# A recurrent attention kernel: weight loading at the start, attention rows kept in SBUF, feed-forward slots shifted by one

## The chip, the cores and the metric

One core of a Trainium2 chip. The metric is device time in microseconds (us) of one launch; the medians below are over several runs. Shorter words used below: PE is TensorE, DVE VectorE, ACT ScalarE, POOL GpSimd, SP SyncE; a "q" behind a name (SPq) is that engine issuing DMAs.

## The reference

A sequence of 2048 rows of width 640 is cut into 64 segments of 32 rows. Each segment attends, in 32 heads of 128, to itself and to 8 memory rows, and the memory rows of its output are the next segment's memory. So the segments form a chain. A feed-forward layer with a squared relu follows; it depends on nothing but its own rows.

```python
for s in range(64):
    h = concat([mem, LN(x)[32*s : 32*s+32]])       # 40 rows
    q, k, v = h @ Wq, h @ Wk, h @ Wv               # 640 -> 32 heads x 128
    o = softmax(mask(q k^T * scale)) v             # 40 x 40 for each head
    o = o @ Wo                                     # 4096 -> 640
    mem = o[:8];  out_a[s] = o[8:]                 # mem goes to the next segment
h  = x + out_a
h2 = h + (relu(LN(h) @ w1 + b1) ** 2) @ w2 + b2    # hidden width 1728
```

Inputs and result are bf16.

## The kernel before

It works in 16 blocks of four segments (128 rows). PE's work in a segment is: projections q, k, v (`ps`), transposes (`pt`), scores (`pss`), softmax sums (`pz`), values (`po`), output projection (`pw`), and the small matmul that puts the new memory into place (`pm`). The last 8 rows of each segment ("tails") are needed by nobody in the chain; a block's tails are projected together (`pst`, `psw`). The feed-forward layer of block b-1 is cut into 8 "slots" (`psf`, `acc`) that fill the places in block b where PE would wait; its transposes are called `pth`.

The weights are laid out in four groups of 160 rows: 128 rows of each group make one full chunk of 128 partitions, and the four remainders of 32 rows together make the fifth chunk. The parts that the change touches:

```python
# start: fifth chunks go DRAM -> DRAM -> SBUF
for wi, src in enumerate((A_Wq, A_Wk, A_Wv)):
    nc.scalar.dma_start(out=w4s[wi].rearrange("(g r) f -> g r f", g=G),
                        in_=src.rearrange("(g q) h e -> g q (h e)", g=G)[:, 128:DG, :])
for wi, (w, src) in enumerate(((wq, A_Wq), (wk, A_Wk), (wv, A_Wv))):
    w2d = src.rearrange("d h e -> d (h e)")
    for c in range(4):
        nc.sync.dma_start(out=w[:, c, :], in_=w2d[c * DG:c * DG + 128, :])
    nc.sync.dma_start(out=w[:, 4, :], in_=w4s[wi])
wov = A_Wo.rearrange("h e d -> e h d")
for j in range(4):
    (nc.sync if j % 2 else nc.scalar).dma_start(out=wo[:, j * 8:(j + 1) * 8, :], in_=wov[:, j * 8:(j + 1) * 8, :])
# ... cut ...
# attention rows of the tails: 16 stores to DRAM for each block, read back by ff_rows
for g in range(G):
    for sp in range(4):
        r0 = b * 128 + sp * SEG + HD
        nc.sync.dma_start(out=a_rows[r0:r0 + TL, g * DG:(g + 1) * DG],
                          in_=ot[32 * g + sp * TL:32 * g + (sp + 1) * TL, :])
# ... cut: step(), the segment; the order of PE's work in it ...
half(wk, lhs, 1, kr, "dve")
run(first[2])
run(slots.get("k", ()))
run_ff("pv3")                                  # one feed-forward slot, or pth
turn(qr, qT[:, :, :, 0:SEG], "act", psum_v, "pv0")
turn(kr, kT[:], "dve", psum_v, "pv1")
# ... cut: scores, softmax ...
run_ff("pv0")                                  # one more slot
# ... cut: values ...
wo_units(lambda h: oT[:, h, 0:SEG], pw, 0, H)
o = wo_out(pw)
for g in range(G):
    nc.sync.dma_start(out=a_rows[s * SEG:s * SEG + HD, g * DG:(g + 1) * DG],
                      in_=o[32 * g + M:32 * g + SEG, :])
mem_to_hT(o, hT4s[(s + 1) // 4], (s + 1) % 4)  # pm
# ... cut ...
# last segment: feed-forward weights of the last block (fw, 4.4 MB) on SyncE's queue
if s == 4 * NB - 1:
    sl["q"].append(last_loads)
```

The softmax here doesn't subtract the row's maximum and nothing guards it: scores larger than these inputs give would overflow.

## Time and profile before

| quantity | value |
|---|---|
| median of the first five runs | 1302.75 us (1302.08 to 1305.56) |
| span of the profiled run | 1300.6 us, mean granted clock of PE 0.978 |
| first output projection (pw of segment 0) starts | 104.87 us |
| segments 1, 8, 60 and 63 start | 109.73, 236.49, 1186.13, 1238.82 us |
| one block in the body (segments 8 to 59, 13 blocks) | 73.05 us |

The page's lines are shown in the prediction.

### The profile page before, as it was taken

The page shows a single profiled execution, that of the slowest core. Times are in us where ns is not written, and L with a number is a line of the kernel's source. Part 1 is how long each engine was busy: PE and PEld are TensorE (multiplying, and loading weights), DVE is VectorE, ACT ScalarE, POOL GpSimd, SP SyncE. Part 2 cuts the span into 40 slices and gives each one's busy share as a digit, 9 for nine tenths or more (in the row PEclk, how much of TensorE's full clock was granted, in tenths as well). Part 3 has the DMA queues.
Part 4 walks back from the last instruction along what each step waited for, and adds up shares of the span by engine and source line. Part 5 has one row for each costly group of instructions (what it writes and reads, how often), then busy time and mean ns, then how long its engine had stood idle before and what let it go on. Part 6 is the DMA issues. An engine that isn't in the chain of part 4 may idle for free. (4 is left out here: it accounts for less than half of the span.)

```text
span 1300.6 us, 68304 instructions
## 1 busy us (share of the span) xinstructions
PE 1090.5 (84%) x31488; PEld 710.6 (55%) x31488; DVE 464.7 (36%) x987; ACT 414.7 (32%) x848; POOL 305.8 (24%) x981
## 2 busy tenths in 40 slices
PE   0058878999999999989999999999999999889865
PEld 0025545656566655656565555656565565556543
DVE  0003333344343434344333433344433434343411
ACT  0012323334343333334333333334333333334312
POOL 3001132222222222222221222222222222222213
PEclk9998989999999999999999999999999999999978
DMA  8840031222222222223222222223222232222250
GB/s 303 326 150 5 6 93 30 78 76 91 63 74 80 75 80 68 72 76 90 63 71 83 76 76 65 79 76 91 67 78 71 75 86 63 69 74 86 77 181 17
DMA packets 97576, 112.55 MB, mean 87 GB/s; under 512 B 30731, under 2 KB 94122, under 8 KB 95322
## 3 DMA queue, kind: packets, MB, share of 16 engines
q1 hardware_dynamic: 94078, 100.19, 25.2%
q8 instruction: 246, 4.03, 1.2%
q10 hardware_dynamic: 2140, 5.77, 1.2%
q0 software_dynamic: 1072, 2.23, 0.6%
q14 instruction: 40, 0.33, 0.1%
HBM read 102.88 MB, written 10.60 MB: 87 GB/s over the span
## 5 line engine op out<-in xcount | busy, mean ns | idle before, releaser
L208 PEld LDWEIGHTS <-hT 128*32 128x32 bf16 x7680 | 205.8, 97 | 185.0 <-issue 8.6
L227 PE MATMUL pw<-wo,oT 128*32 128x160 bf16 x8192 | 169.5, 239 | 44.4 <-issue 40.9
L227 PEld LDWEIGHTS <-oT 128*32 128x32 bf16 x8192 | 150.9, 100 | 67.2 <-issue 48.2
L208 PE MATMUL ps<-wv,hT 128*32 128x512 bf16 x2560 | 163.5, 383 | 0.0
L381 POOL TENSOR_TENSOR f<-ffr 128x128 bf16<-128x128 bf16 x224 | 84.7, 398 | 328.5 <-ACT ffr L379 277.6
L208 PE MATMUL ps<-wq,hT 128*32 128x512 bf16 x2560 | 155.0, 388 | 6.4 <-DVE hT L287 6.1
L208 PE MATMUL ps<-wk,hT 128*32 128x512 bf16 x2560 | 150.2, 380 | 0.0
L129 DVE CAST vr<-ps 128x512 bf16<-128x512 f32 x128 | 88.6, 692 | 71.9 <-PE ps L208 68.7
L379 ACT ACTIVATE ffr<-psf,b1f 128x128 bf16<-128x128 f32 x224 | 69.1, 359 | 91.8 <-PE psf L358 90.0
L129 DVE CAST qr<-ps 128x512 bf16<-128x512 f32 x64 | 44.3, 692 | 141.7 <-PE ps L208 141.7
L232 DVE CAST o<-pw 128x160 bf16<-128x160 f32 x64 | 20.8, 325 | 183.4 <-PE pw L227 173.3
L358 PE MATMUL psf<-hnT,w1c 128*128 128x128 bf16 (+1 forms) x1020 | 76.2, 220 | 9.5 <-DMA w1c<-w1d 9.5
L127 ACT COPY qT<-pt 128x1024 bf16<-128x1024 bf16 x64 | 64.8, 1012 | 58.1 <-PE pt L220 58.1
L451 POOL TENSOR_TENSOR p<-p,mask_t 128x128 bf16<-128x128 bf16 x64 | 27.5, 429 | 224.4 <-ACT p L444 224.4
L129 DVE CAST oT<-po 128x320 bf16<-128x320 f32 x128 | 56.9, 486 | 64.5 <-PE po L486 58.1
L127 ACT CAST qr<-ps 128x512 bf16<-128x512 f32 x64 | 37.5, 586 | 122.6 <-PE ps L208 122.6
L127 ACT CAST tq<-pst 128x512 bf16<-128x512 f32 x32 | 18.9, 591 | 178.2 <-PE pst L208 178.2
L358 PEld LDWEIGHTS <-w1c 128*128 128x128 bf16 (+1 forms) x1020 | 60.6, 99 | 26.6 <-issue 11.9
L370 PE MATMUL acc<-w2c,f 128*128 128x320 bf16 x404 | 72.8, 301 | 0.9 <-DMA w2c<-in_B_w_dram 0.8
L127 ACT CAST kr<-ps 128x512 bf16<-128x512 f32 x64 | 37.5, 586 | 102.5 <-PE ps L208 102.5
L127 ACT CAST oT<-po 128x320 bf16<-128x320 f32 x128 | 48.2, 429 | 68.3 <-PE po L486 68.3
L467 POOL TENSOR_TENSOR pn<-p,rk 128x128 bf16<-128x128 bf16 x64 | 42.8, 668 | 107.4 <-issue 80.8
(97 smaller groups left out, 1375.4 us busy)
## 6 DMA issues: line engine op xcount, KB each, us to landing
w1c<-w1d SPq DMA_DIRECT2D x190, 160.0 KB
w2c<-in_B_w_dram SPq DMA_DIRECT2D x188, 160.0 KB
wq<-in_A_Wq_dram SPq DMA_DIRECT2D x4, 1024.0 KB
wk<-in_A_Wk_dram SPq DMA_DIRECT2D x4, 1024.0 KB
wv<-in_A_Wv_dram SPq DMA_DIRECT2D x4, 1024.0 KB
a_rows<-o SPq DMA_DIRECT2D x256, 7.5 KB
a_rows<-o SPq DMA_DIRECT2D x256, 2.5 KB
xt<-in_A_x_dram SPq DMA_DIRECT2D x16, 160.0 KB
```

The costliest lines, as they stand in the source:

```text
L127: nc.scalar.copy(out=out_, in_=in_)
L129: nc.vector.tensor_copy(out=out_, in_=in_)
L208: nc.tensor.matmul(ps[32 * g:32 * g + 32, :], lhsT=lhs(c), rhs=w[:, c, g * EG + n * 512:g * EG + (n + 1) * 512], start=(c == 0), stop=(c = ...
L227: nc.tensor.matmul(ps[32 * g:32 * g + 32, 0:DG], lhsT=lhs(h), rhs=wo[:, h, g * DG:(g + 1) * DG], start=(h == 0), stop=(h == H - 1))
L232: nc.vector.tensor_copy(out=o[:], in_=ps[:, 0:DG])
L358: nc.tensor.matmul(ps[0:fs, j, :], lhsT=w1c[:, c, 0:fs], rhs=f["hnT"][:, c, :], start=(c == 0), stop=(c == DC - 1))
L370: nc.tensor.matmul(f["acc", hf][:, 0:320], lhsT=t1[0:k, :], rhs=w2c[0:k, hf * 320:(hf + 1) * 320], start=(fc == 0), stop=(fc == FC - 1))
L379: nc.scalar.activation(out=r[0:fs], in_=ps[0:fs, j, :], func=ACT.Relu, bias=b1f[0:fs, fc:fc + 1], scale=1.0)
L381: nc.gpsimd.tensor_tensor(out=t1[0:fs], in0=r[0:fs], in1=r[0:fs], op=ALU.mult)
L451: nc.gpsimd.tensor_tensor(out=p[:, :, NQ:NC], in0=p[:, :, NQ:NC], in1=mask_t[:, sp].unsqueeze(1).to_broadcast([128, HG, M + TL]), op=ALU.mult)
L467: nc.gpsimd.tensor_tensor(out=pn[:, :, NQ:NC].rearrange("p i (a q) -> p i a q", q=M), in0=p[:, :, NQ:NC].rearrange("p i (a q) -> p i a q", ...
```

## The change

Its intent: start the chain earlier, take single waits of PE away, and keep attention rows in SBUF instead of sending them through DRAM. Six parts, the diff cut to its core (left out: the loads of w1c and w2c are issued later within a segment, the last step of the feed-forward layernorm, `ff_apply`, moved from behind the q to behind the k projection, and some tail units are split otherwise):

```diff
@@ 1. start
-        for wi, src in enumerate((A_Wq, A_Wk, A_Wv)):
-            nc.scalar.dma_start(out=w4s[wi].rearrange("(g r) f -> g r f", g=G), ...)
+        load_x(1)                                  # second x block ahead of the weights
         ...
-            nc.sync.dma_start(out=w[:, 4, :], in_=w4s[wi])
+            for g in range(G):
+                nc.sync.dma_start(out=w[g * DR:(g + 1) * DR, 4, :], in_=w2d[g * DG + 128:(g + 1) * DG, :])
         ...
+        for j in (1, 3):
+            load_wo(j, nc.sync)                    # quarters 0 and 2: gpsimd, after the second block's transposes
@@ 2. attention rows
-                                nc.sync.dma_start(out=a_rows[r0:r0 + TL, g * DG:(g + 1) * DG],
-                                                  in_=ot[32 * g + sp * TL:32 * g + (sp + 1) * TL, :])
+                            stores.append(lambda eng, g=j // 4, sp=j % 4: eng.dma_start(
+                                out=rows_of(b)[sp * SEG + HD:(sp + 1) * SEG, g * DG:(g + 1) * DG], in_=...))
+                    sl["w"].append(lambda: run_stores(8, (nc.gpsimd,)))       # first segment of a block
+                        sl["q"].append(lambda b=b: (run_stores(8, (nc.gpsimd,)), ff_rows(b - 1)))   # second
@@ 3. w1 reformatted into w1d: ten GpSimd DMAs after block 0 become two in each of segments 0 to 6
+                for fc in range(2 * s, min(2 * s + 2, FC)):
+                    sl["w0"].append(lambda fc=fc: nc.gpsimd.dma_start(out=w1d[fc, :, :, 0:fs_of(fc)], ...))
@@ 4. feed-forward: pth behind pw of the third segment, slots one place later
-                        ffq.append(lambda tag, b=b: ff_turn(b - 1))
+                        sl["f"] = [lambda b=b: ff_turn(b - 1)]
+                    if sp == 3:
                         ffq.extend(lambda tag, b=b, p=p: ff_slot(b - 1, p, tag) for p in range(NP + 1))
@@ 5. fw: all its loads from sync to gpsimd
-                    sl["q"].append(last_loads)
+                    sl["k"].append(last_loads)
@@ 6. tail of the last block
-        ff_rows(NB - 1)
+        run_stores(16, (nc.sync, nc.scalar, nc.gpsimd))
-        for k in range(len(ffq)):
+        for k in range(2):
             run_ff(tags[k % 2])
         ff_stats(NB - 1)                           # its root now on ScalarE (Ln, Exp)
         ff_apply(NB - 1)
+        while ffq:
+            run_ff(tags[len(ffq) % 2])
         ff_turn(NB - 1)
```

## The prediction

> **What bounds the kernel now.** I read the page first, then the waits of TensorE (PE), then the order in time at the start, at one seam near 170 us and at the end. The page's busy shares and slices:
>
> ```profile
> PE 1090.5 (84%) x31488; PEld 710.6 (55%) x31488; DVE 464.7 (36%) x987; ACT 414.7 (32%) x848; POOL 305.8 (24%) x981
> PE   0058878999999999989999999999999999889865
> DMA  8840031222222222223222222223222232222250
> ```
>
> PE is busy 84%, every other engine under half. A slice is 32.5 us: PE is empty for two slices, nine tenths busy through the body, and sinks at the end. The body is a chain of 64 dependent segments, so only time in which PE stands still can be won. Who PE waits for, in total, times and longest:
>
> ```profile
> PE ptx L196 <- DVE xn L122: 58.4, 3, 33.3
> PE pw L227 <- issue: 40.9, 37, 1.7
> PE pth L343 <- DVE hn L122: 19.1, 15, 9.9
> PE pst L208 <- DMA wq<-w4s: 17.7, 1, 17.7
> ...
> PE psw L227 <- issue: 10.3, 9, 2.0
> PE psf L358 <- DMA w1c<-w1d: 9.5, 1, 9.5
> ...
> PE pss L437 <- POOL qT L416: 5.5, 1, 5.5
> ```
>
> Several are single events, so I placed them in time. The start:
>
> ```profile
> 53.43 0.89 DVE L105 BATCH_NORM_STATS2 lnst<-xt 128x6 f32<-128x320 bf16 x2 [27.28 <-DMA xt<-in_A_x_dram]
> ...
> 79.18 2.75 PE L208 MATMUL pst<-wq,hTt 128*32 128x512 bf16 x24 [17.71 <-DMA wq<-w4s]
> ```
>
> The second x block arrives at 53.4, because its load is queued behind all weights. Then PE does 16 matmuls and waits until 79.2 for the fifth chunk of wq, which goes DRAM to DRAM (w4s) and then into SBUF. The first output projection (pw) starts at 104.87. The seam after block 0, and the end:
>
> ```profile
> 163.67 1.25 POOL L589 DMA_DIRECT2D w1d<-in_B_w_dram  x1
> ...
> 172.56 0.39 PE L437 MATMUL pss<-qT,kTt 128*32 128x16 bf16 x32 [5.48 <-POOL qT L416]
> ```
>
> ```profile
> 1258.14 1.25 PE L358 MATMUL psf<-hnT,w1c 128*128 128x128 bf16 x10 [9.52 <-DMA w1c<-w1d]
> ...
> 1268.84 5.34 SPq L276 DMA_DIRECT2D a_rows<-o  x16
> ...
> 1278.46 0.49 DVE L328 TENSOR_TENSOR ffh<-ffa,ffh 128x640 bf16<-128x640 bf16 x1 [2.94 <-issue]
> ...
> 1284.60 0.71 PE L343 MATMUL pth<-ident,hn 128*128 128x128 bf16 x5 [9.86 <-DVE hn L122]
> ```
>
> Ten DMA issues on GpSimd hold up its copy of qT, and PE with it. In the last segment a small w1c load stands behind 4.4 MB of fw in the same queue. At the very end the attention rows travel to DRAM (16 stores of 0.33 us each) and back before the last layernorm can start, and its root takes 12 short GpSimd operations.
>
> **What the Trainium skill says.** "DMA: Bandwidth & Descriptors", section on why a DMA increments its semaphore by 16: the engines that share a transfer number the largest count up to 16 that divides the slowest dimension. The old w4s copy has 4 there, so 4 engines. The transfers of the first 60 us, in slices of 1.5 us, fit: the rate collapses around 13 to 17 us although megabytes are waiting, and reaches 410 to 437 later.
>
> ```profile
> GB/s 0 284 246 368 259 296 473 337 193 33 98 24 273 410 415 431 431 415 426 421 431 437 410 415 431 415 426 385 370 375 363 363 362 292 97 256 4 320 295 392
> ```
>
> "SBUF — State Buffer", section "Door 1: The DMA port swizzle": 32 partitions reach only 8 of 16 ports, measured 189 GB/s at 1 MiB. The new loads of the fifth chunks are 32 rows each. No transfer of the kernel before shows this. "DMA: Bandwidth & Descriptors", section "Queues, rings and completion order": an engine goes round robin between the queues, packet by packet. So fw on GpSimd's queue no longer stands ahead of w1c on SyncE's, it shares with it; the 9.5 us wait shows the old queueing. "Runtime: NRT & Kernel Launch", section "Instruction fetch mechanics": instructions come in 16 KiB blocks of 256. The page has 246 instruction packets for 4.03 MB, 16.4 KB each, and the places of the "pw <- issue" gaps, counted in PE's instructions, keep nearly one remainder of 256 from a gap to the next. The change keeps PE's instructions (62,978 before and after), so these some 51 us stay.
>
> **The change part by part.**
>
> 1. Start. Removed: the w4s copies, and the DRAM round trip of three fifth chunks. The second x block is loaded first. Two wo quarters move from ScalarE's queue to GpSimd's. PE's start: from the first bias cast (19.1) to the first layernorm's transposes took 5.6 us and the second x block needs some 6 more, so PE starts at 31 us, or as early as 25 if the bias lands sooner on engines that w4s no longer clogs. The wq work takes some 10 us (1.9 + 8.5 from the timeline), the wk work 8, two transposes 1. So PE wants wv at 44 to 50 us. When does it arrive? Bytes in queue order: xt 0.33 MB and three times 5.24 MB. At 0.42 MB/us the 12.9 MB of full-width loads take 31 us. The 3.15 MB of 32-row loads at an assumed 0.2 MB/us (estimate from the skill's SBUF page) take 16 us. With 2.5 us to start and some 3 us given to the two wo quarters, wv is complete near 53. From wv's fifth chunk to pw is some 8 us (95.53 to 104.87 before, less 1.0 for two transposes now done earlier). The last wo quarter should be in at about 60. So pw of segment 0 starts near 61 instead of 104.87: minus 44.
>
> 2. Seam at 170 us. The ten w1d issues (9 us together) become two per segment, after the oTt copy, where GpSimd is idle for several us. Minus 5.5, and minus 1 because the matmuls after the stall ran on a lowered clock (24 wv matmuls in 2.75 against 1.49 us).
>
> 3. Body, 14 blocks. The feed-forward transposes (pth) leave the place where they waited for hn and go behind pw in the third segment, and all slots of the feed-forward shift by one. PE's work is the same. Of 19.1 us of waits 9.9 are the last one, so 9.2 in 14 times, 0.65 each, vanish; the 0.3 us of transposes then lies inside the wait for the o copy (0.42 at that spot). Given back: the hnT eviction (0.49 us) on VectorE gets ahead of the hT copy, about +0.25, and the third segment keeps 8 instead of 12 filler matmuls ahead of pw, about +0.2. Net about 0.5 to 0.7 a block, minus 8. The 16 tail stores move to GpSimd in two lots of 8: at 0.54 us an issue (its small w1d issues) 4.3 us a lot, in stretches where GpSimd waits 5 us and more. I take nothing for them. Attention rows stay in SBUF; that was hidden, nothing.
>
> 4. Last segment. fw goes through GpSimd's queue (about 5 us of issue at 0.55 and 1.13 us apiece, finished before GpSimd's next mask). w1c shares the engines with fw: 640 KB at half of 0.4 MB/us and 2 us to land, against 5 us of room, so a wait of 0 to 2 us stays. pw then also runs at full clock (3.98 against 2.40 us). From its first matmul to the eviction of pw the segment takes 26.8 us now (1238.82 to 1265.65), the one before it 15.8 (1222.02 to 1237.83): 11.0 lost, of which I expect 9 back.
>
> 5. Tail. 16 stores over three queues (5 or 6 each, 2 to 3 us) straight into the SBUF tile, no reload; root by two ScalarE operations of about 0.25 us each instead of 3.8 us. From the end of the tail projection, 0.5 to evict, 2.7 to issue, 2 to land, 1.6 for add and statistics, 0.6 for the root: 7.5. But ScalarE's program order puts the root ahead of the relus of the slots that remain, so four slots follow it: 4.3 us, and pth starts at 11.8 after that point, before at 16.2. Minus 4.4.
>
> Sum: 44 + 6.5 + 8 + 9 + 4.4 = 72 to 74. 1302.75 minus 73.5 gives **1229 us**.
>
> **Rivals.** First: the start is bound by something else. For it: 21.4 MB (weights, wo and x) must come through the same engines, nothing here makes that less than 51 us at 0.42. If the 32-row loads run at full rate, pw starts near 55 and the total is 1223. If they are slower than half, or the bias load on GpSimd's queue (12.2 us to land before) gets still slower behind the denser weights, pw starts near 70: 1238. Against a late bias: PE has 3 to 9 us to spare before wv is complete. Second: GpSimd becomes the new wait, with 16 more issues a block and fw ahead of the mask in the last segment. For: the 5.48 us stall above shows that it can. Against: its idle time before the mask is 224 us over 64 segments. If each lot delayed PE by 0.5 us the body would give back 14 us: 1243. Third: instruction refills get worse where the DMA is busy, in the start and the last segment: some 3 us more, 1232. Fourth: the body wins nothing, because a removed wait for hn only uncovers the next refill: 1237.
>
> **Range and chances.** The start may miss by 6 to 9 either way, the body by 8, the rest by 4; taken as independent some 12. Range 1215 to 1243. Within 2% means above 1276.7: that would need the start to win under a third of its 44 with all else failing. Faster 0.97, same 0.02, slower 0.01.
>
> **What would show it.** In the profile after: PE's first pst near 25 to 31 without a 17 us gap; a wait on wv that ends near 53; pw of segment 0 at 61; a dip in the GB/s row in each 32-row load; no wait on qT near the end of block 0; no wait of pth on hn in the body; "pw <- issue" about as before; w1c at the end under 2.5 us; pth of the last block at 12 us behind the tail projection. It is wrong if pw of segment 0 starts beyond 70, or if waits on GpSimd's copies appear in every block.

## More of the kernel before

A segment's start is read from the order in time: it is the first of its q projections. Differences between such starts divide the span into stages, and each stage can be compared between two kernels by itself.

## The result, and the profile after

The changed kernel takes 1240.2 us (median of 9 runs, 1236.15 to 1243.66) against 1302.7 us (16 runs, 1298.57 to 1305.68) for the kernel before in the same rounds: a ratio of 0.9515, 95% interval 0.9499 to 0.9532. A ratio here is always the mean time of one kernel's fast runs over that of the other's of the same rounds, so it is not quite the ratio of the medians. The profiled run of the changed kernel happens to be its slowest (1243.66); its span is 1242.0 us. So a stage table from the two profiles adds up to 58.6 us, where the medians differ by 62.5.

| stage (from the starts of segments) | before | after | difference |
|---|---|---|---|
| start of the span to segment 1 | 109.73 | 77.80 | -31.9 |
| segments 1 to 3 | 50.07 | 49.74 | -0.3 |
| segments 4 to 7 (block 1) | 76.69 | 68.19 | -8.5 |
| segments 8 to 59 (13 blocks) | 949.64 | 935.20 | -14.4 |
| segments 60 to 62 | 52.69 | 55.14 | +2.5 |
| segment 63 to the end of psw | 29.6 | 25.3 | -4.3 |
| end of psw to pth of the last block | 16.2 | 15.2 | -1.0 |
| pth to the end | 16.0 | 15.5 | -0.5 |

The page, PE's busy share and its slices:

```profile
PE 1089.6 (88%) x31488; PEld 711.1 (57%) x31488; DVE 468.3 (38%) x988; ACT 415.8 (33%) x850; POOL 436.6 (35%) x1226
PE   1578898999989999999999999999989989998876
```

PE does the same 31,488 matmuls in the same busy time (1090.5 before). Its share rises only because it stands still for less time. POOL has 131 us more to do (305.8 before), of which 122.8 are its new stores. PE's waits in the changed kernel (total, times, longest):

```profile
PE pw L236 <- issue: 47.1, 37, 2.2
...
PE psw L236 <- issue: 12.3, 9, 1.9
PE pst L217 <- DMA wv<-in_A_Wv_dram: 10.1, 3, 4.5
...
PE psf L377 <- DMA w1c<-w1d: 6.1, 2, 4.4
...
PE pst L217 <- DMA wk<-in_A_Wk_dram: 4.2, 1, 4.2
...
PE pm L304 <- DVE o L241: 2.2, 5, 0.4
```

The wait for the first x blocks (ptx on xn) fell from 58.4 to 26.5 us. Gone are the waits on w4s (17.7), of pth on hn (19.1), of pss on GpSimd's qT (5.5). New are the waits on wk and wv at the start. The gaps named "issue" ahead of pw and psw, which the prediction takes for instruction refills, come 46 times in both profiles, not at the same places, and their sum grew from 51.2 to 59.4 us. It moves from run to run, though: the unedited changed kernel has 56.3 us in another profile (after_again), and a kernel with the same body 51.5 (w4s_back). So a cost of the change is not shown here. Two of the waits at the start, in the order in time:

```profile
42.40 2.75 PE L217 MATMUL pst<-wk,hTt 128*32 128x512 bf16 x24 [4.23 <-DMA wk<-in_A_Wk_dram]
...
64.46 1.90 PE L217 MATMUL pst<-wv,hTt 128*32 128x512 bf16 x16 [4.03 <-DMA wv<-in_A_Wv_dram]
```

Two more waits on wv lie before 64.46; the one shown is the last, and it ends when the fifth chunk of wv is there. The transfers of the first 80 us, in slices of 2 us:

```profile
GB/s 13 156 266 414 398 381 202 414 258 225 234 401 418 426 418 400 240 231 250 232 303 392 401 390 404 400 418 295 217 202 239 351 364 362 324 58 18 0 150 101
```

The three dips (about 16 to 22 us, 32 to 42 us, 54 to 62 us) are the three sets of 32-row loads. Full chunks run at 390 to 426 GB/s and these at 202 to 303. The end of the last segment and the tail:

```profile
1199.81 0.71 PE L377 MATMUL psf<-hnT,w1c 128*128 128x128 bf16 x5 [4.36 <-DMA w1c<-w1d]
...
1205.24 3.88 PE L236 MATMUL pw<-wo,oT 128*32 128x160 bf16 x128 [0.54 <-ACT oT L134]
...
1211.75 4.04 ACTq L296 DMA_DIRECT2D ffa<-o  x5
...
1215.90 0.63 ACT L399 ACTIVATE ffr<-psf,b1f 128x128 bf16<-128x128 f32 x2 [10.38 <-DMA ffa<-o]
...
1219.17 0.49 DVE L347 TENSOR_TENSOR ffh<-ffa,ffh 128x640 bf16<-128x640 bf16 x1 [7.45 <-DMA ffa<-o]
...
1226.52 0.44 PE L362 MATMUL pth<-ident,hn 128*128 128x128 bf16 x5
```

w1c is still waited for (4.36 us here, 1.77 once more), and pw behind it still runs on a lowered clock (0.58 granted from 1205.2 to 1209): 3.88 us, where 128 such matmuls take 2.40 at full clock. In the tail, ACT's five stores hold it for 4.04 us, so the relus of the remaining slots start only at 1215.90; all rows are in SBUF at 1219.17, 7.8 us behind the end of psw (1211.33). SyncE's share of the rows was issued last: its six stores start only at 1212.68, behind the four stores of the segment's other rows, and take until 1217.50. hn is ready at 1221.87; PE still has slots ahead of pth in its order, and pth starts at 1226.52.

One cost is small but instructive. The same store of attention rows costs more time to issue when its destination is SBUF. Groups by tile; the three numbers before the times are the shortest, the median and the longest issue in ns. First the kernel before, then the changed one:

```profile
L501 SPq DMA_DIRECT2D a_rows<-o x256: 289/362/1865, 109.1 to 1267.2; - x128
L276 SPq DMA_DIRECT2D a_rows<-o x256: 263/293/1625, 181.1 to 1273.9; - x128
```

```profile
L527 SPq DMA_DIRECT2D ffa<-o x256: 713/722/1339, 80.9 to 1211.9; - x128
L296 POOL DMA_DIRECT2D ffa<-o x245: 499/500/836, 143.9 to 1214.0; - x123
L296 SPq DMA_DIRECT2D ffa<-o x6: 624/624/665, 1212.7 to 1216.9; - x6
```

A head store doubles from 0.362 to 0.722 us, and a tail store on SyncE from 0.293 to 0.624.

### The profile page after: what moved, and what is told of

Same layout as the page of the kernel before. It is cut to its first block, busy times and chain, and to the rows that moved or that the text cites. A ratio compares the mean times of both kernels' runs of the same rounds, so it can differ in the third digit from the quotient of the medians.

```text
span 1242.0 us, 68483 instructions
## 1 busy us (share of the span) xinstructions
PE 1089.6 (88%) x31488; PEld 711.1 (57%) x31488; DVE 468.3 (38%) x988; ACT 415.8 (33%) x850; POOL 436.6 (35%) x1226
## 4 chain that ended last, share of the span: by engine, by line
PE 77%; issue 7%; DMA 6%; DVE 5%; ACT 3%; POOL 1%; SPq 0%; POOLq 0%; DVEq 0%; ACTq 0%
PE ps L217 31%; PE pw L236 13%; PE pst L217 7%; PE pt L229 5%; PE psf L377 5%; PE acc L389 3%; PE psw L236 3%; PE po L506 2%; DMA wv<-in_A_Wv_dram 2%; PE po L512 2%; DMA wk<-in_A_Wk_dram 2%; DVE vr L136 2%; PE pz L483 1%; DVE pn L492 1%; PE pss L467 1%
## 5 line engine op out<-in xcount | busy, mean ns | idle before, releaser
L217 PE MATMUL ps<-wq,hT 128*32 128x512 bf16 x2560 | 150.0, 379 | 7.1 <-DVE hT L308 6.8
L296 POOL DMA_DIRECT2D ffa<-o x245 | 122.8, 518 | 16.1 <-issue 7.4
L136 DVE CAST kr<-ps 128x512 bf16<-128x512 f32 x64 | 44.3, 692 | 76.3 <-PE ps L217 76.3
```

The costliest lines, as they stand in the source:

```text
L136: nc.vector.tensor_copy(out=out_, in_=in_)
L217: nc.tensor.matmul(ps[32 * g:32 * g + 32, :], lhsT=lhs(c), rhs=w[:, c, g * EG + n * 512:g * EG + (n + 1) * 512], start=(c == 0), stop=(c = ...
L296: stores.append(lambda eng, g=j // 4, sp=j % 4: eng.dma_start(out=rows_of(b)[sp * SEG + HD:(sp + 1) * SEG, g * DG:(g + 1) * DG], in_=ot[32 ...
```

## The experiments

Twelve kernels ran. Four were timed in three rounds, eight in five, each against the kernel before on the same chip. They are all the changed kernel with one edit, except for after_again, which is unedited, and the combined one. Between calls the changed kernel's own ratio moved from 0.9515 to 0.9556, some 5 us, so smaller differences are read within one call, or from the stages. Stages move as well: in the eleven profiles whose kernels have the body of the changed one, segments 8 to 59 took 925.2 to 936.1 us, and segments 60 to 62 took 52.5 to 57.5. "Fifth chunk" below is the 32-row remainder of each group.

| kernel | median us | ratio to before (95%) | pw of segment 0 | segment 63 to end of psw | end of psw to pth |
|---|---|---|---|---|---|
| changed kernel | 1240.2 | 0.9515 (0.9499 to 0.9532) | 73.61 | 25.3 | 15.2 |
| ch4_ports | 1228.43 | 0.9457 (0.9412 to 0.9503) | 62.87 | 24.8 | 14.1 |
| ch4_pool | 1238.61 | 0.9522 (0.9482 to 0.9561) | 68.81 | 25.3 | 14.4 |
| wo_sync | 1231.92 | 0.9479 (0.9437 to 0.952) | 64.42 | 24.4 | 13.9 |
| w4s_back | 1267.71 | 0.9751 (0.9713 to 0.9789) | 103.22 | 25.2 | 16.1 |
| after_again | 1240.29 | 0.9556 (0.9529 to 0.9583) | 73.39 | 24.8 | 15.1 |
| fw_after | 1232.63 | 0.9511 (0.9485 to 0.9536) | 72.44 | 19.4 | 15.3 |
| tail_order | 1233.53 | 0.9513 (0.9488 to 0.9538) | 73.89 | 25.2 | 13.3 |
| body_undo | 1247.54 | 0.9617 (0.9591 to 0.9643) | 72.90 | 25.2 | 13.8 |
| ch4_step4 | 1226.56 | 0.9443 (0.9419 to 0.9468) | 62.42 | 24.8 | 15.1 |
| ch4_both | 1229.38 | 0.9465 (0.9441 to 0.949) | 65.80 | 24.8 | 13.9 |
| best | 1224.26 | 0.9434 (0.9412 to 0.9457) | 59.03 | 19.6 | 14.0 |
| stores_sync | 1293.62 | 0.9955 (0.9932 to 0.9977) | 73.77 | 25.3 | 14.3 |

The first four ran in one call, the next four in a second, the last four in a third. Kernels with fifth chunks in the wrong rows (ch4_ports, ch4_step4) still passed the comparison, because these inputs make that part of the result small against the tolerance.

### The start: why pw came 12 us later than predicted

**ch4_ports: the fifth chunk over 128 partitions.**

```diff
-            for g in range(G):
-                nc.sync.dma_start(out=w[g * DR:(g + 1) * DR, 4, :], in_=w2d[g * DG + 128:(g + 1) * DG, :])
+            for j in range(4):
+                nc.sync.dma_start(out=w[:, 4, j * 1024:(j + 1) * 1024], in_=w2d[0:128, j * 1024:(j + 1) * 1024])
```

> The changed kernel with each weight's fifth chunk loaded by four transfers of 256 KB that span all 128 partitions (2 KB a row) instead of four of 32 partitions (8 KB a row). The rows are the wrong ones, so the result is wrong on purpose; bytes, queue and order stay. Theory 1 (a 32-partition transfer moves at about half rate): the dips to 200 to 250 GB/s in the start vanish, wv is complete near 54 us instead of 64.4, the first pw starts near 63 instead of 73.6, the time falls by some 10 us against the changed kernel (ratio to before near 0.944). Theory 2 (the dips come from the two wo quarters on GpSimd's queue, or from many small transfers): dips and the start of pw stay, time within 2 us of the changed kernel (ratio 0.9515).

pw started at 62.87. In the row of transfers the dips are gone: from 14 us to the end of the weights no slice of 2 us is below 372 GB/s until 52 us, and the wo quarters after that run at 361 to 366. So the narrow loads, and not the amount of data, hold the start back by some 11 us. That run changes two things, though: which partitions are written, and how long each row is.

**ch4_step4: 32 rows as before, on every fourth partition.** This separates the two: same rows, same row length, same number of loads; only the partitions differ.

```diff
-                nc.sync.dma_start(out=w[g * DR:(g + 1) * DR, 4, :], in_=...)
+                nc.sync.dma_start(out=w[g:g + 125:4, 4, :], in_=...)
```

> The fifth chunks as in the changed kernel, four loads of 32 rows for each weight, same sizes, same queue, but each load puts its rows on every fourth partition (0, 4, 8 ... and so on) instead of 32 neighbours, so that each reaches all 16 ports of SBUF by the table in the skill's SBUF page. The rows then lie wrong: a wrong result on purpose. If the ports are the reason for the dips, they vanish (all slices before 34 us at 390 or more, as with the 128-partition chunks) and pw of segment 0 starts near 63. If 32 rows are slow for another reason (few packets for each engine, row length), the dips at 200 to 260 stay and pw starts at 71 to 76.

The dips vanish again, and pw starts at 62.42. The row of transfers, slices of 2 us from 0:

```profile
GB/s 14 156 274 426 394 360 226 414 422 422 426 422 414 430 414 412 392 401 392 383 402 391 406 391 413 379 363 363 361 357 86 8 82 145 27 86 12 8 0 0
```

Compare its places 9 to 11 (422 422 426) with those of the changed kernel (258 225 234): the same 256 KB loads at the same place in the same queue. On the average of these three slices, 32 neighbouring partitions get 57% of the rate of 32 spread ones (239 of 423). This is what "SBUF — State Buffer" of the Trainium skill, in the section that the prediction names, says of its 16 ports; the measured dips lie above its 189 GB/s.

**ch4_pool: the narrow loads of wk and wv on GpSimd's queue, beside SyncE's full chunks.** The idea: if a narrow load uses half the ports, a full-width load beside it could use the rest.

```diff
-            for g in range(G):
+            for g in range(G if wi == 0 else 0):
                 nc.sync.dma_start(out=w[g * DR:(g + 1) * DR, 4, :], in_=...)
         ...
+        for w, src in ((wk, A_Wk), (wv, A_Wv)):        # before wo quarters 0 and 2
+            for g in range(G):
+                nc.gpsimd.dma_start(out=w[g * DR:(g + 1) * DR, 4, :], in_=...)
```

> The changed kernel with the 32-row transfers of wk and wv issued by GpSimd, ahead of its two wo quarters, so that they run beside full-width weight loads on SyncE's queue; right result, same bytes. Theory 1 (half rate because 32 partitions leave half of the memory's ports unused): full-width packets fill what the narrow ones leave, so the rate stays above 300 GB/s and pw starts 4 to 9 us earlier than 73.6; ratio near 0.946. Theory 2 (the sum of bytes through a common rate, whatever the partitions): pw starts within 2 us of 73.6, ratio 0.9515.

```profile
GB/s 12 158 262 422 394 380 206 418 258 225 213 410 426 414 414 373 258 258 250 262 246 246 262 258 259 378 395 390 379 363 358 355 365 361 360 169 120 167 17 4
```

The whole stream runs at 246 to 262 GB/s for 18 us: the full chunks are slowed as well (from 32 to 50 us SyncE's queue moved 2.63 MB and GpSimd's 1.93 MB). The holes are not filled. pw came 5 us earlier, of which 2.2 us are left at segment 8, and the time is that of the changed kernel (ratio 0.9522).

**ch4_both: all narrow loads first, two groups from SyncE and two from ScalarE at once.** A version with right results.

```diff
+        for w, src in ((wq, A_Wq), (wk, A_Wk), (wv, A_Wv)):      # ahead of the full chunks
+            for g in range(G):
+                (nc.sync if g < 2 else nc.scalar).dma_start(out=w[g * DR:(g + 1) * DR, 4, :], in_=...)
```

> A right kernel: the fifth chunks of all three weights come first, groups 0 and 1 from SyncE's queue and groups 2 and 3 from ScalarE's at the same time; together they reach all ports. If ports are the reason: the first 10 us run near 400, PE's start stays near 28, pw of segment 0 at 60 to 65, ratio to the kernel before 0.943 to 0.949. If narrow loads are slow whatever runs beside them: 13 to 15 us at 200 to 260 at the very start, PE's first matmuls 5 us later, pw at 67 to 74.

```profile
GB/s 12 258 188 249 259 264 194 197 262 397 418 434 406 442 406 430 414 395 405 392 398 385 402 390 394 408 420 370 364 360 364 352 74 8 131 119 90 12 8 0
```

Here the ports theory, as I had stated it for this run, failed: two loads at once, in groups that together reach both halves of the ports, still ran at 188 to 264 GB/s for 14 us, a mean of 230, though both queues moved data (by 15 us 1.64 MB came through SyncE's and 1.36 MB through ScalarE's). By the port table of the same SBUF page all 16 ports were in reach of the two together. But the same page says, in its section "Can I just issue two DMAs to hit both halves?", that two DMAs at once, one in each half, gain only 6% over one; the run agrees with that, and my expectation had overlooked it. The run is faster than the changed kernel all the same (ratio 0.9465; PE starts 3.5 us later, pw 7.8 us earlier), because the slow stretch now lies before PE starts, and PE has room there.

**wo_sync: all of wo on SyncE's queue, behind the weights.**

```diff
-        for j in (1, 3):
+        for j in range(4):
             load_wo(j, nc.sync)
         ...
-        for j in (0, 2):
-            load_wo(j, nc.gpsimd)
```

> The changed kernel with all four wo quarters on SyncE's queue behind the weights, none on GpSimd's. Theory 1 (32-row loads are slow by themselves): the dips stay at the same depth but carry weights alone, so wv is complete some 4 to 6 us before 64.4, and pw then waits for wo: it starts within 4 us of 73.6. Theory 2 (the competing wo quarters make the dips): the dips vanish and pw starts at 66 or earlier.

pw started at 64.42 instead of 73.6; PE's last wait on wv ended at 54.71 instead of 64.46. I had expected at most 4 us. The dips stayed, down to 206 to 229 GB/s, so the two wo quarters do not make them. But in the changed kernel GpSimd's wo quarters share the engines with wk and wv, which are wanted first. After pw's start PE waits 2.4 us for the last wo quarter, so segment 1 starts 6.2 us earlier (71.61 against 77.80). My 3 us for this share in the prediction was a third of what it took (9.75 at the arrival of wv).

**w4s_back: the old staging put back, the early x block kept.**

```diff
+        for wi, src in enumerate((A_Wq, A_Wk, A_Wv)):
+            nc.scalar.dma_start(out=w4s[wi].rearrange("(g r) f -> g r f", g=G), in_=...)
         ...
-            for g in range(G):
-                nc.sync.dma_start(out=w[g * DR:(g + 1) * DR, 4, :], in_=...)
+            nc.sync.dma_start(out=w[:, 4, :], in_=w4s[wi])
```

> The changed kernel with the old staging of the fifth chunks through DRAM (three copies from ScalarE's queue, then one full-width load each); everything else of the change stays, so the second x block still comes early. If the staging is what held PE at the start, the first pw starts 20 us or more later than 73.6 and most of the 31 us won there is lost (ratio near 0.97). Rival: the early x block is the gain and the staging costs little: pw within 6 us of 73.6, ratio below 0.957.

```profile
PE pst L220 <- DMA wq<-w4s: 45.4, 1, 45.4
```

pw is back at 103.22, within 2 us of the kernel before. So nearly the whole gain of the start needs the staging to go, and the earlier x block alone gains almost nothing: that only moves the wait from x to w4s. Whether dropping the staging would do without the early x block was not run. This run also keeps every other part of the change, and still gains 2.5%: the two halves of the change, start and rest, are about equal.

### The body

**after_again** is the changed kernel, unedited, as the reference for the next three.

> The changed kernel once more, beside the next three on the same chip: ratio 0.9515 within 0.003. It is what the next three are compared with.

Its ratio of 0.9556 is above that range; its median is the same (1240.29). The kernel before ran faster in this call (1296.19).

**body_undo: pth back between the slot and the transposes of q in the third segment; all else kept.**

```diff
             run_ff("pv3")
+            run(slots.get("k2", ()))
             turn(qr, qT[:, :, :, 0:SEG], "act", psum_v, "pv0")
         ...
-                        sl["f"] = [lambda b=b: ff_turn(b - 1)]
+                        sl["k2"] = [lambda b=b: ff_turn(b - 1)]
```

> The changed kernel with the feed-forward transposes put back between the first slot and the transposes of q in every third segment, so that only their new place is undone. Theory: their new place hides them in the wait for the o copy; undone, PE again waits for o there (0.42 a block) and spends 0.3 to 0.5 us on the transposes in the open, but hn is ready in time because its layernorm was applied as early as before, so pth waits 0.3 us or more; 1 us a block, 10 to 16 us in all: ratio 0.960 to 0.964. Rival: the shift of the slots alone won the body's 14 us, and the place of the transposes matters under 0.3 us a block: ratio under 0.955.

+0.0061 in the ratio, some 7.9 us, under the 10 to 16 us expected; the ratio itself lies in its range, since after_again's is higher than I had reckoned with. PE's wait for o in the kernel before, then two lines of this run (in the changed kernel the wait for o is 2.2 us, 5 times, and that for hn is absent):

```profile
PE pm L283 <- DVE o L232: 8.6, 20, 0.4
```

```profile
PE pm L304 <- DVE o L241: 8.6, 20, 0.4
...
PE pth L362 <- DVE hn L129: 1.8, 2, 1.5
```

pm waits again for the copy of o, 0.4 us in each block: behind pw, the transposes had filled just that. The wait for hn did not come back in the body. hn is not made earlier: in block 8 it is ready 5.99 us after the start of the third segment here, 5.72 in the kernel before. But a whole slot stands ahead of pth now, which starts at 6.04 us and has nothing to wait for; so this is not the old kernel's order. PE's waits in segments 8 to 59 split the body's gain of 14.4 us. Gone are 7.2 us of pth on hn and 3.4 us of po on pn (6.7 to 3.3), which this run keeps, and 5.6 us of pm on o, which it gives back. PE's busy time fell by 4.9 us and the issue gaps grew by 5.7; both move by about as much between kernels with the same body. That the shift of the slots took away the first two is read from the order of the instructions, not from a run of its own.

**stores_sync: the 16 tail stores of each block on SyncE instead of GpSimd.**

```diff
-                    sl["w"].append(lambda: run_stores(8, (nc.gpsimd,)))
+                    sl["w"].append(lambda: run_stores(8, (nc.sync,)))
         ...
-                        sl["q"].append(lambda b=b: (run_stores(8, (nc.gpsimd,)), ff_rows(b - 1)))
+                        sl["q"].append(lambda b=b: (run_stores(8, (nc.sync,)), ff_rows(b - 1)))
```

> The changed kernel with the 16 tail stores of each block on SyncE instead of GpSimd (the last block's as they are). I took nothing for them on GpSimd, so by my theory the time stays within 3 us of the changed kernel (ratio 0.951 to 0.957), and PE's waits on GpSimd's copies stay at zero. By the rival (GpSimd's 122 us of issue work delay the body), it is over 5 us faster. The third possibility: SyncE's issues of 0.6 to 0.7 us delay its w1c and w2c loads, PE then waits on w1c or w2c in the blocks, and it is slower by 3 us or more.

The third possibility, and far stronger than I had written: ratio 0.9955, which gives back 52 to 57 us (0.040 to 0.044 of 1298). Two of PE's waits, and the order in time at one seam, first SyncE's issues, then what PE does at the end of them:

```profile
PE psf L377 <- DMA w1c<-w1d: 37.1, 18, 3.9
...
PE acc L389 <- DMA w2c<-in_B_w_dram: 5.5, 14, 0.8
```

```profile
588.22 6.07 SPq L296 DMA_DIRECT2D ffa<-o  x9
594.39 3.02 SPq L527 DMA_DIRECT2D ffa<-o  x4
597.45 4.67 SPq L296 DMA_DIRECT2D ffa<-o  x7
602.23 0.85 SPq L323 DMA_DIRECT2D w1c<-w1d  x2
...
604.58 0.94 PE L377 MATMUL psf<-hnT,w1c 128*128 128x128 bf16 x10 [2.07 <-DMA w1c<-w1d]
```

20 stores in a row hold SyncE for 14 us, and the load of the next w1c stands behind them. A block takes 75.62 us instead of 71.94. The waits on w1c and w2c are 37 us over the changed kernel's 6.1; the rest lies in PE's own pace (1116 us busy against 1090, mean clock 0.959 against 0.977). In the kernel before, 16 such stores to DRAM took 16 times 0.293, 4.7 us; with SBUF as their destination they take 16 times 0.624, 10.0 us. So the two halves of the second part belong together: rows kept in SBUF on the old queue would have cost nearly all that the rest of the change wins, and GpSimd has the room.

### The last segment and the tail

**fw_after: fw in two parts on GpSimd, both after the small w1c loads.**

```diff
             run_ff("pv3")
+            run(slots.get("k2", ()))                 # first part of last_loads (w1)
         ...
-                    sl["k"].append(last_loads)
+                    sl["k2"] = [last_loads]
+                    sl["d"].append(last_w2)          # second part (w2)
```

> The changed kernel with the 4.4 MB of fw still on GpSimd's queue but issued in two parts behind the first feed-forward slot of the last segment, so that the last two w1c loads go out ahead of them. Theory: the 6.1 us that PE waits for w1c there is sharing of the engines with fw, and its lowered clock afterwards (pw in 3.9 instead of 2.4 us) follows from it. Then w1c waits under 1 us, pw takes 2.4 us, and the time falls by 5 to 8 us against the changed kernel (ratio near 0.946). Rival: the bytes of fw are on the path anyway, and the wait comes back as a wait for fw at the first slot behind the tail projection: less than 2 us won.

-0.0045, some 5.8 us. The wait on w1c is gone, pw runs at full clock, and from segment 63 to the end of psw the kernel takes 19.4 us instead of 24.8. All kernels that issue fw as the changed one does take 24.4 to 25.3 us there; this one and best take 19.4 and 19.6. A new gap stands behind psw:

```profile
1197.92 2.40 PE L236 MATMUL pw<-wo,oT 128*32 128x160 bf16 x128 [0.56 <-ACT oT L134]
...
1208.65 0.50 PE L377 MATMUL psf<-hnT,fw 128*128 128x128 bf16 x3 [3.67 <-issue]
```

The trace calls it "issue" and names no load of fw. Counted in PE's instructions, it stands at the same remainder of 256 as the gaps ahead of pw in the blocks before it. The changed kernel has 0.26 us at that place, when its fw had landed; here fw was still coming in until 1206, at some 350 GB/s. That fits the prediction's third rival, refills that get longer where the DMA is busy, but no run tested it, and pth comes no later for it (15.3 against 15.1 us).

Changing only the queue of fw, as the change does, lets w1c share the engines with 4.4 MB. What it needed was the order.

**tail_order: last stores without ScalarE, four slots instead of two ahead of the last statistics.**

```diff
-        run_stores(16, (nc.sync, nc.scalar, nc.gpsimd))
+        run_stores(16, (nc.sync, nc.gpsimd))
         ...
-        for k in range(2):
+        for k in range(4):
             run_ff(tags[k % 2])
```

> The changed kernel with the last 16 stores issued by SyncE and GpSimd only, none by ScalarE, and with four feed-forward slots instead of two ahead of the last layernorm in program order. Theory: in the changed kernel ScalarE issues its five stores in 4 us and its relus wait behind them, then its root holds up the relus of the later slots while it waits for the rows; freed of both, the four slots fill that time, and the last feed-forward starts 2 to 4 us earlier behind the tail projection than the 15.2 us of the changed kernel; ratio near 0.949. Rival: the eight stores per queue land later by as much as is won, within 1 us of the changed kernel.

pth came 13.3 us behind the end of psw, 1.8 us under after_again. But kernels with an unchanged tail show 13.8 to 16.1 in the table above, so one profile can't carry this difference. By time it is 0.0043 faster, 5.6 us, more than that stage could give; in the trace segment 63 also starts 4 us earlier, where the kernels are the same. I take the gain of the tail order as not shown.

### All together

**best**: fifth chunks as in ch4_both, wo as in wo_sync, fw as in fw_after, tail as in tail_order. Results right by construction as well as by the comparison.

> The right version made of what has paid so far: fifth chunks as in the run before this one, all of wo on SyncE behind the weights, fw in two parts after the small w1c loads, last stores on two queues and four slots ahead of the last statistics. If the gains add (start 12 us, last segment 5, tail 2 to 4): 18 us under the changed kernel, ratio 0.935 to 0.943, some 1217 to 1226 us. If they collide at the end (both move the same wait), the two together give only 5 us and the ratio is 0.941 to 0.947.

0.9434, 1224.26 us: the fastest right kernel here, 16 us under the changed one by medians of different calls (10 to 16 by the ratios), and 74 us under the kernel before of its own call (1298.15). Its ratio misses the range for gains that add by 0.0004 and lies in that for gains that collide; its time lies in the 1217 to 1226 us given for gains that add. The stages say where. Segment 63 to the end of psw is 19.6, so fw's 5 us are there. End of psw to pth is 14.0, where ch4_both, with the old tail, had 13.9: the tail order gave nothing. And of pw's 14.6 us at the start (59.03 against 73.61) only 8.9 are left at segment 8 (186.84 against 195.73). In part PE waits 2.5 us for wo inside pw. In ch4_step4, too, 11.0 us at segment 1 become 7.6 at segment 8. In segments 1 to 3 the granted clock was 0.90 in ch4_step4, 0.95 in best and 0.93 in the changed kernel, so the clock does not explain both; why the gain shrinks is open.

## Why the prediction was right

1229 (1215 to 1243) was said; 1240.2 was measured, in the range and 11 us above the point. The main claim held: PE's standing still at single places is what the change removes, above all at the start. Most sizes were off, in both directions, and that the body made up for part of what the rest lacked was luck.

| step of the prediction | said | measured | shown by |
|---|---|---|---|
| start, to pw of segment 0 | -44 (104.87 to 61) | -31.3 (to 73.61) | stages; ch4_ports, ch4_step4, wo_sync |
| seam after block 0 | -6.5 | -6.6 in segment 4 (25.83 to 19.27) | stages |
| body | -8 | -14.4 in 13 blocks, -2 more in block 1 | stages; PE's waits; body_undo |
| segments 60 to 62 | 0 | +2.5 | within the scatter of this stage |
| last segment, first matmul to the eviction of pw | -9 | -3.7 (26.8 to 23.1) | stages; fw_after |
| tail, end of psw to pth | -4.4 | -1.0 | stages only |

- **Start.** The mechanism was right: w4s_back shows that the staging held PE, and PE's first matmul on wq came at 28.18, inside the 25 to 31 that was said. The term that was mis-sized is the arrival of wv, 53 in the prediction and 64.46 in the trace. The rate taken for the narrow loads was not the error: 0.2 MB/us was assumed and 0.24 came in the first dip. Its 3 us for the two wo quarters were: they cost wv 9.75 us (wo_sync), and they share the engines inside the two later dips; the dips last some 24 us in all instead of 16. A smaller part is the first 14 us, which brought 3.7 MB (sum of the slices), where 0.42 MB/us from 2.5 us on would make 4.8. My own criterion, "wrong if pw of segment 0 starts beyond 70", was met; that the total stayed in the range is owed to the body, whose extra 8 us I had given no reason for. One of the nine runs (1243.66) lies outside.
- **Seam.** Right in size. Segment 4 no longer waits for GpSimd's qT (5.5 us); no run undid this part by itself.
- **Body.** pth's wait on hn vanished as said (7.2 us in segments 8 to 59), and behind pw the transposes hide the wait for o (5.6 us there, 0.43 a block instead of 0.3). But the step had the wrong cause for the first: in body_undo the wait for hn stays away without the new place, with a slot ahead of pth. I had given the shift of the slots only costs (hnT's eviction, thinner filler) and no gain, and it also comes with 3.4 us less of po's wait on pn. The fourth rival did not come true: the gaps called "issue" took back 0.3 to 9 us in the kernels with this body, not all of the gain.
- **Segments 60 to 62.** Not in the prediction, and not shown to come from the change. pw of segment 62 takes 4.04 us instead of 2.40 in the profile of the changed kernel. But ch4_ports, ch4_pool, w4s_back and tail_order, which have the same code there, ran it in 2.40, and six others, after_again among them, in 3.85 to 4.04. What decides it is open.
- **Last segment.** "A wait of 0 to 2 us stays" was wrong by 4: 6.1 us stay, and with them pw's low clock. The step that failed is that w1c would get half of 0.4 MB/us beside fw. From 1194 to 1200 us SyncE's queue got 0.32 MB and fw's 1.86 MB: 280 packets against 362, but packets of 1.1 KB against 5.1 KB. So sharing packet by packet came out near half of the packets and 15% of the bytes. fw_after shows that the wait is worth 5 us and that order removes it.
- **Tail.** The root on ScalarE came as predicted. So did the slots that follow it (hn ready to pth: 4.65 us, 4.3 said). The mis-sized term is the stores: on SyncE and ScalarE they take 0.62 to 0.67 us each (I took 0.5), and SyncE's six started 1.35 us behind the end of psw and took 4.8 us with the gaps between them. Their rows landed 7.8 us behind the end of psw instead of 5.2. Whether ScalarE's five stores, which hold up its relus, cost anything stays open (tail_order).
- **Rivals.** The first (the start is bound otherwise) is what happened, at 73.6, even beyond the 70 it allowed. The second, GpSimd as the new wait, did not: there is no wait of PE on a GpSimd copy in the body, with 122 us of store issues on it. stores_sync shows the other side, that SyncE had no such room. The third, refills that get longer where the DMA is busy, was not tested; the gap of 3.67 us in fw_after fits it.
- **Slips in the working**, none of which moves the range: the five terms add up to 71.9, not to 72 to 74 (1230.8 us instead of 1229); a result within 2% needs the start to win under 26 of its 44 us if all else wins nothing, not under a third; the root before has 14 short GpSimd operations, not 12.

## What to carry to other kernels

Before you count bytes, ask which partitions a load writes: 32 neighbours ran at 57% of the rate of 32 spread ones, and they slowed every load beside them too. A queue that feeds the critical engine has room for only so many issues, and the price of an issue changes with its destination; moving stores is worth checking by the time their queue stays blocked, not by their bytes. And when a wait is behind a large load, move the large load after the small one; another queue alone leaves them sharing.

## What the Trainium skill lacked or had wrong

- "SBUF — State Buffer", section on the DMA port swizzle: it agrees with loads taken one after the other (225 to 258 GB/s in the first dip on 32 neighbouring partitions, 422 and more on 32 spread ones). What no page states for loads into a core's own SBUF: that a narrow load slows full-width loads of another queue as well (246 to 262 GB/s in all for 18 us). That two narrow loads at once in different port halves do not add up, it does say; here they made 188 to 264 GB/s for 14 us.
- "Runtime: NRT & Kernel Launch", section "Instruction fetch mechanics": it calls the crossing of a 16 KiB block mostly hidden, and gives no figure for a crossing that is not. PE has 62,976 instructions here, so 246 blocks. The gaps called "issue" ahead of pw and psw were 51 us before and 59 us after, 46 of them in both, so 1.1 and 1.3 us each, at about one crossing in five. That they are refills is an inference from their places, as the prediction tells; no run took them away.
- No page that I found: the time to issue a small store on SyncE into SBUF, 0.62 to 0.72 us in this kernel, against 0.29 to 0.36 us into DRAM.
